# Attention block gated by a Mish MLP, one core: W1's last 18 tiles split beside the MLP's first chunk, attention's due times stretched there, a fourth buffer for Q/K results

## The chip, the cores and the metric

The kernel runs on one core of one Trainium2 chip. Five engines work from queues of their own: TensorE (PE: matmuls, PEld: weight loads), VectorE (DVE), ScalarE (ACT), GpSimd (POOL) and SyncE (SP, which issues most DMAs). The metric is device time in microseconds. The kernel before has three runs: 3395.11, 3398.99 and 3401.33 us, median 3398.99.

## The reference

```python
xn = layernorm(x)                                   # x: 1 x 2048 x 1024
q, k, v = split(xn @ wqkv)                          # 32 heads of 32
p = softmax(q @ k.T * 32 ** -0.5)                   # 2048 x 2048 for each head
s = concat(p @ v) @ wo
h = xn @ w1 + b1                                    # 1024 x 3584
g = silu((h * tanh(softplus(h))) @ w2)              # Mish between the two products
return x + s * g
```

All inputs are float32. The kernel keeps float32's precision by splitting each operand into a high and a low fp32r part: high is a copy that rounds, low is the difference. Three products (high high, high low, low high) are added up, so each logical product takes three matmuls.

## The kernel before

**Stages.** The layer norm, its transposes and V's products come first (to about 203 us). Then Q/K: 16 column blocks q = 0 to 15, seven products of 12 matmuls each (a scheme that needs seven products of halves in place of eight), whose results go through `qst` tiles to DRAM (`qs`, `ks`). Then attention and the MLP run interleaved (from about 558 us), and the output product `op` closes the program (from 3216 us).

**W1.** W1 has 28 tiles of 128 columns, each of 1024 rows in two halves. The MLP works on four chunks of 512 rows of x, so every tile is used four times: tile n of 112 is column tile n % 28. A tile is loaded in float32, split into high and low, and stored split to DRAM (`w1s`); `load_w1` loads it from there, 1 MB. The buffer ring `w1` has two places. In the kernel before, all 28 tiles are split ahead of the MLP:

- `W1_V` = 10 tiles in the V stage: `w1_early` loads one (`w1e`), and POOL makes both parts (`w1p`). It is called at ten of the V stage's steps and at two of those after it.
- the other 18 in Q/K: `presplit` takes half a tile at a time, 36 jobs, at three of the seven products of a block, except in blocks 6 to 8. It loads `praw`; three products later POOL casts it to `pw` and subtracts; one product later SP stores it to `w1s`.

**POOL in Q/K.** Besides those jobs, POOL makes the sums of Wqkv's halves (`ws`), and from the eleventh block on the low part of every second weight piece `wq`. It takes all of this in program order. TensorE's product waits for the low part of its `wq` at its third matmul.

**xr** is a 512-row operand of the products. It is loaded in four parts from `ts` just as Q/K starts. SP issues its DMAs in program order, too.

**Attention and MLP.** The order is made by a planner (`Plan`) when the kernel is built. It has a list of operations for each engine with an assumed duration, needs and buffer rings, and steps through a model of time; the order in which it issues them is the fixed order of each engine's queue on the chip. TensorE takes, of the operations that are ready, the one with the earliest due time, its `key`. Attention's keys (`s`, `t`, `pv`) run on `slot` for each step T (a head has 16 steps, 512 in all); the MLP's (`h`, `y`) on `tile_time` for each of the 112 tiles. `LEAN` is a string of digits, one for each 21 us of the model's time, that shifts keys by kind.

In a step of attention, TensorE makes `s` (for the row maxima, DVE `mx`) and `t` (transposed scores); ACT makes `p` = exp(t); POOL adds the p tiles up in `z`, which TensorE sums up in `zp` at the head's end; `pv` is the product with V. Seven `p` buffers lie between ACT and POOL. The head's result goes through one buffer, ring `on`, tag `on0`: ACT copies it there from PSUM, DVE scales it, SP stores it (`ot`) in four parts.

In the MLP, `h` takes 24 matmuls for a tile, the Mish goes over ACT and DVE, `y` takes another 24. W2 is split in the first chunk by `w2_op`: SP loads `w2r`, ACT makes the high part, POOL the low part, SP stores both (`w2s`); 56 of these half tiles.

Of the kernel before, what the change touches and what calls it, by code (L numbers as in the profile page):

```python
# [18 lines left out]
P = 128  # L19
# [7 lines left out]
W1_V = 10  # L27
# [23 lines left out]
LEAN = ("22007810058567756445438735813771770600785277035346426643654653488"  # L51
        "67323135577524547706646266273377660776675018744007005760023872000")
# [176 lines left out]
def body(ctx: ExitStack, tc: tile.TileContext, x, wqkv, wo, w1, b1, w2, out):  # L229
# [264 lines left out]
    for t in range(2, NT + 2):  # L494
# [32 lines left out]
        if t > 3 and t % 3:  # L527
            w1_early()
# [80 lines left out]
    for i, t in enumerate([4, 5, 6, 7, 12, 13, 14, 15, 0, 1, 2, 3, 8, 9, 10, 11]):  # L609
        v_group(1, t)()  # L610
        if i in (1, 3):
            w1_early()
# [107 lines left out]

    jobs = iter([(f, half) for f in range(W1_V, FT) for half in range(2)])

    def presplit():
        job = next(jobs, None)
        if job is None:
            return
        f, half = job
        raw = sp.tile([P, 512], F32, tag="praw", name=f"praw{f}_{half}", bufs=2)
        w = sp.tile([P, 2, 512], F32R, tag="pw", name=f"pw{f}_{half}", bufs=2)
        nc.sync.dma_start(raw.rearrange("p (k f) -> p k f", f=P),  # L730
                          w1[half * 512:half * 512 + 512, f * P:(f + 1) * P].rearrange("(k p) f -> p k f", p=P))

        def split():
            nc.gpsimd.tensor_copy(w[:, 0], raw)
            low(nc.gpsimd, w[:, 1], raw, w[:, 0])

        later.at(3, split)
        later.at(4, lambda: move(w1s[f][:, :, half * 4:half * 4 + 4], w.rearrange("p a (k f) -> p a k f", f=P)))
# [22 lines left out]
    def out_(q, half, chunk_, src):  # L761
        st = sp.tile([P, 2, 512], F32R, tag="qst", name=f"qst{q}_{half}_{chunk_}", bufs=3)
# [42 lines left out]

    q_load(1, ring_of(1))
    x_load(xr, ts[4])
# [71 lines left out]


# [6 lines left out]
    def s_stream():  # L887
        for h in range(1, H):
# [3 lines left out]
            for qt in range(NT):  # L892
                for kc in range(4):
# [10 lines left out]
                    m = Op("PE", MM, key=slot * (16 * (h - 1) + qt + (kc + 1) / 4 - LEAD), need=[loaded[h]],  # L904
# [59 lines left out]
    def t_stream():  # L964
        pts = {}
        for T in range(NS):
# [4 lines left out]
            for c in range(4):  # L971
# [14 lines left out]
                m = Op("PE", MM, key=slot * (T + (c + 1) / 4), emit=mm, take=["t", "b"], kind="t",  # L986
# [30 lines left out]
    def product(T, pts, size):  # L1017
# [18 lines left out]
        last_pv[h] = op("PE", PV * size, key=slot * (T + 1.5), need=need + [vt_[h]], emit=emit, col=True, kind="pv",  # L1036
# [52 lines left out]
    xts_ = {0: xc0}  # L1089

    def w1_op(n):
        def emit(at):
            load_w1(n)
        w1_ops[n] = op("SP", 0.1, emit=emit, take=["w1"], bytes_=P * 2 * KT * P * 4)
# [50 lines left out]
    def h_stream():  # L1145
        for n in range(NC * FT):
# [7 lines left out]
            for k in range(KT):  # L1154
                for a, b in THREE:
                    def mm(at, n=n, c=c, k=k, a=a, b=b, i=i, t=t):
                        if i == 0:
# [6 lines left out]
                           need=([w1_ops[n]] if n else []) + ([xc_ops[c, k // 2 * 2]] if c else []),  # L1164
# [342 lines left out]
```

## Time and profile before

| | |
|---|---|
| median of the three runs | 3398.99 us |
| the profiled execution: its own time | 3396.45 us |
| its span, first to last instruction | 3394.7 us |
| granted TensorE clock, mean | 0.996 |
| TensorE busy | 3354.4 us |
| POOL busy | 2556.3 us |
| DMA moved | 531.97 MB, mean 157 GB/s |

The profile is one execution. A line of the table of stretches has the stretch, its length, then for each engine busy us and instructions in brackets, the granted clock, the share of the DMA engines and GB/s. A line of the timeline has its start and length in us, engine, line, operation, output<-inputs and count; in square brackets stands how long the engine sat idle before it, and what ended that. A line of the groups has busy us, mean ns of one, then the idle time ahead of them and what ended it. The names are the program's, with numbers left out.

### The profile page before, as it was taken

How to read it: one execution, taken by the hardware profiler on the slowest of the kernel's cores; microseconds unless marked ns; L12 is line 12 of the kernel's file. 1: busy time of each engine (PE TensorE's matmuls, PEld its weight loads, DVE VectorE, ACT ScalarE, POOL GpSimd, SP SyncE). 2: the span in 40 equal slices, each digit the busy share in tenths (PEclk: the TensorE clock that was granted, in tenths of full speed). 3: DMA queues.
4: the chain of work that ended last, by engine and by line, in shares of the span. 5: the costliest groups of instructions: out<-in, count | busy, mean ns of one | idle time of the engine just before them, and what ended most of it. 6: DMA issues, size and time to landing. Idle time of an engine off the chain costs nothing.

```text
span 3394.7 us, 45896 instructions
## 1 busy us (share of the span) xinstructions
PE 3354.4 (99%) x16867; PEld 2460.3 (72%) x16867; DVE 2551.6 (75%) x3988; ACT 2037.3 (60%) x3272; POOL 2556.3 (75%) x789
## 2 busy tenths in 40 slices
PE   8999989999999999999999999999999999999999
PEld 7878767677777767777777777777777767777787
DVE  6776667887788777787788877878887787886543
ACT  5333324666766667666666676666676666666621
POOL 2445455899998999988888788888887888888800
PEclk9999999999999999999999999999999999999999
DMA  7978977434344463334333533343445343333482
GB/s 254 358 266 284 299 246 218 145 119 150 119 150 140 128 209 105 110 115 125 100 110 116 194 105 117 108 128 103 122 118 188 117 119 119 106 118 118 140 294 87
DMA packets 305732, 531.97 MB, mean 157 GB/s; under 512 B 88714, under 2 KB 151690, under 8 KB 283018
## 3 DMA queue, kind: packets, MB, share of 16 engines
q1 hardware_dynamic: 285796, 487.36, 45.8%
q10 hardware_dynamic: 19712, 41.69, 3.3%
q8 instruction: 133, 2.18, 0.3%
q14 instruction: 91, 0.75, 0.1%
HBM read 378.76 MB, written 149.16 MB: 156 GB/s over the span
## 4 chain that ended last, share of the span: by engine, by line
PE 91%; DMA 2%; DVE 2%; ACT 1%; issue 1%; POOL 0%; SPq 0%; ACTq 0%; DVEq 0%; POOLq 0%
PE y L1249 18%; PE h L1159 17%; PE t L978 14%; PE s L896 13%; PE pv L1025 13%; PE op L1348 5%; PE q_y L784 3%; PE v L351 2%; PE q_x L784 2%; PE q_z L784 2%; PE zp L1051 1%; DMA xc<-ts 1%; DVE mx L686 0%; DVE mx L902 0%; DMA w2r<-in_B_w_dram 0%
## 5 line engine op out<-in xcount | busy, mean ns | idle before, releaser
L1007 POOL TENSOR_TENSOR z<-z,p 128x2048 f32<-128x2048 f32 x448 | 2067.8, 4616 | 148.7 <-ACT p L282 123.1
L282 ACT ACTIVATE p<-t,zero 128x512 f32<-128x512 f32 x2048 | 1374.6, 691 | 502.2 <-PE t L978 481.6
L902 DVE TENSOR_REDUCE mx<-s 128x1 f32<-128x512 f32 x1984 | 1325.0, 686 | 420.6 <-PE s L896 412.3
L1249 PE MATMUL y<-w,act 128*128 128x512 f32 x2688 | 926.1, 391 | 2.2 <-ACT p L282 2.1
L978 PE MATMUL t<-qstack,kstack 128*128 128x512 f32 x2048 | 798.8, 393 | 0.9 <-DMA qstack<-mt 0.6
L896 PE MATMUL s<-kstack,qstack 128*128 128x512 f32 x1984 | 772.4, 393 | 0.8 <-DVE mx L902 0.5
L1159 PE MATMUL h<-xr,w 128*128 128x512 f32 x2016 | 702.6, 391 | 0.0
L1249 PEld LDWEIGHTS y<-w,act 128*128 128x128 f32 x2688 | 503.8, 188 | 111.5 <-issue 2.5
L978 PEld LDWEIGHTS t<-qstack,kstack 128*128 128x128 f32 x2048 | 383.0, 188 | 114.8 <-issue 22.0
L1025 PE MATMUL pv<-p,v 128*32 128x512 f32 x4096 | 459.2, 594 | 0.0
L896 PEld LDWEIGHTS s<-kstack,qstack 128*128 128x128 f32 x1984 | 370.2, 188 | 116.6 <-issue 24.5
L1159 PEld LDWEIGHTS h<-xr,w 128*128 128x128 f32 x2016 | 378.0, 188 | 81.1 <-issue 3.4
L1025 PEld LDWEIGHTS pv<-p,v 128*32 128x32 f32 x4096 | 123.8, 110 | 284.2 <-issue 282.1
L1271 DVE TENSOR_TENSOR yacc<-yacc,y 128x512 f32<-128x512 f32 x416 | 282.8, 681 | 38.1 <-PE y L1249 37.1
L1007 POOL TENSOR_TENSOR z<-p,p 128x2048 f32<-128x2048 f32 x32 | 147.8, 4620 | 184.8 <-PE zp L1051 145.8
L1159 PE MATMUL h<-xc,w 128*128 128x512 f32 x672 | 224.8, 391 | 0.1
L351 PE MATMUL v<-vw,xc 128*128 128x512 f32 x768 | 180.8, 394 | 1.5 <-DVE vw L293 1.5
L351 PEld LDWEIGHTS v<-vw,xc 128*128 128x128 f32 x768 | 143.1, 189 | 33.1 <-DVE vw L293 3.1
L1159 PEld LDWEIGHTS h<-xc,w 128*128 128x128 f32 x672 | 125.9, 188 | 26.5 <-ACT p L282 0.4
L784 PE MATMUL q_y<-xc,wq 128*128 128x512 f32 x480 | 122.0, 405 | 11.6 <-POOL wq L293 7.8
L285 ACT ACTIVATE act<-h 128x512 fp32r<-128x512 f32 x112 | 66.7, 595 | 102.2 <-DVE h L1208 100.7
L784 PEld LDWEIGHTS q_y<-xc,wq 128*128 128x128 f32 x480 | 93.9, 196 | 32.8 <-POOL wq L293 8.3
(140 smaller groups left out, 2989.3 us busy)
## 6 DMA issues: line engine op xcount, KB each, us to landing
w<-w1s SPq DMA_DIRECT2D x112, 1024.0 KB, 6.0
w<-w2s SPq DMA_DIRECT2D x168, 512.0 KB, 4.0
w2s<-w SPq DMA_DIRECT2D x56, 512.0 KB, 4.8
qstack<-qs SPq DMA_DIRECT2D x96, 256.0 KB, 6.9
kstack<-ks SPq DMA_DIRECT2D x96, 256.0 KB, 6.1
w1s<-pw SPq DMA_DIRECT2D x36, 512.0 KB, 3.4
qs<-qst ACTq DMA_DIRECT2D x32, 512.0 KB, 3.1
ks<-qst ACTq DMA_DIRECT2D x32, 512.0 KB, 4.8
```

What stands on the lines that cost most here:

```text
L282: nc.scalar.activation(out_, in_, fn, bias=zero if bias is None else bias, scale=scale)
L351: nc.tensor.matmul(ps, xc[t // 4][k // HK][:, a, k % HK, (t % 4) * P:(t % 4 + 1) * P], vw[i, k // 2][:, b, k % 2], start=n == 0, stop=n == ...
L784: nc.tensor.matmul(ps, w[:, a, k], xx[:, b, k], start=m == 0 and i in (0, 1, 4), stop=m == 3 * HK - 1, skip_group_check=i not in (0, 1, 4))
L896: nc.tensor.matmul(sp_, qst[h % 3][:, qt * P:(qt + 1) * P], kst[h % 3][:, kc * 512:(kc + 1) * 512], start=True, stop=True)
L902: nc.vector.reduce_max(tiles["mx"][:, qt, kc:kc + 1], tiles[qt, kc], axis=AX.X)
L978: nc.tensor.matmul(tp, kst[h % 3][:, kt * P:(kt + 1) * P], qst[h % 3][:, c * 512:(c + 1) * 512], start=True, stop=True)
L1007: nc.gpsimd.tensor_tensor(zs[h], pts[T - 1] if kt == 1 else zs[h], pts[T], ALU.add)
L1025: nc.tensor.matmul(pv[h][c * DH:(c + 1) * DH, :], vt[h][:, k, :], pts[T - kt + k][:, c * 512:(c + 1) * 512], start=k == 0, stop=k == NT - 1)
L1159: nc.tensor.matmul(t["h"], w1t[n][:, a, k], xts_[c][k // HK][:, b, k % HK], start=i == 0, stop=i == 3 * KT - 1)
L1249: nc.tensor.matmul(t["y"], acts[n][:, p, s * P:(s + 1) * P], w2t[m_][:, q], start=j == 0 and i == 0, stop=j == YB - 1 and i == 2)
L1271: nc.vector.tensor_tensor(ya, ya, t["y"], ALU.add)
L1348: nc.tensor.matmul(ps[t, dh], ohl[t // 4, k][:, a, s * P:(s + 1) * P], wt[k][:, b, r], start=k == 0 and i == 0, stop=k == KT - 1 and i == 2)
```

## The change

Four things. `W1_V` goes from 10 to 4, so that the V stage splits four tiles at six steps; `presplit` does the tiles 4 to 9, 12 half tiles, all in blocks 0 to 3, with one `pw` buffer in place of two. The tiles 10 to 27 are split by `w1_op` in the MLP's first chunk, half a tile at a time: SP loads 256 KB to the buffer of the heads' outputs (`on0`, now also `w1r`), ACT makes the high part in the tile itself, POOL the low part, and once both halves are through, SP stores the tile to `w1s` for the three chunks that follow. The tile's first use needs no load from `w1s`. `h` waits for each half apart.

Attention's keys go through `due`: below 600 us of the model's time they are stretched by 1.25, and the rest is pressed together so that the end stays. `LEAN` has new digits.

`qst` gets four buffers, three before. And `xr` is loaded ahead of block 1's raw weights instead of behind them.

```diff
-W1_V = 10
+W1_V, W1_Q = 4, 10
+
+SLOW, UNTIL = 1.25, 600.0
...
-LEAN = ("22007810058567756445438735813771770600785277035346426643654653488"
-        "67323135577524547706646266273377660776675018744007005760023872000")
+LEAN = ("17005811310607050748168705630685764600685277038346416663654556688"
+        "64343135546528545608186210263377657666375628744007405708070872000")
...
-        if t > 3 and t % 3:
+        if t > 3 and t % 3 == 2:
             w1_early()
...
-        if i in (1, 3):
+        if i == 1:
             w1_early()
...
-    jobs = iter([(f, half) for f in range(W1_V, FT) for half in range(2)])
+    jobs = iter([(f, half) for f in range(W1_V, W1_Q) for half in range(2)])
...
-        w = sp.tile([P, 2, 512], F32R, tag="pw", name=f"pw{f}_{half}", bufs=2)
+        w = sp.tile([P, 2, 512], F32R, tag="pw", name=f"pw{f}_{half}", bufs=1)
...
-        st = sp.tile([P, 2, 512], F32R, tag="qst", name=f"qst{q}_{half}_{chunk_}", bufs=3)
+        st = sp.tile([P, 2, 512], F32R, tag="qst", name=f"qst{q}_{half}_{chunk_}", bufs=4)
...
+    x_load(xr, ts[4])
     q_load(1, ring_of(1))
-    x_load(xr, ts[4])
...
+    def due(T):
+        t = slot * T
+        if t < UNTIL:
+            return t * SLOW
+        return UNTIL * SLOW + (t - UNTIL) * (total - UNTIL * SLOW) / (total - UNTIL)
...
-                    m = Op("PE", MM, key=slot * (16 * (h - 1) + qt + (kc + 1) / 4 - LEAD), need=[loaded[h]],
+                    m = Op("PE", MM, key=due(16 * (h - 1) + qt + (kc + 1) / 4 - LEAD), need=[loaded[h]],
...
-                m = Op("PE", MM, key=slot * (T + (c + 1) / 4), emit=mm, take=["t", "b"], kind="t",
+                m = Op("PE", MM, key=due(T + (c + 1) / 4), emit=mm, take=["t", "b"], kind="t",
...
-        last_pv[h] = op("PE", PV * size, key=slot * (T + 1.5), need=need + [vt_[h]], emit=emit, col=True, kind="pv",
+        last_pv[h] = op("PE", PV * size, key=due(T + 1.5), need=need + [vt_[h]], emit=emit, col=True, kind="pv",
...
+    w1r, w1_kept = {}, {}
 
     def w1_op(n):
         def emit(at):
             load_w1(n)
-        w1_ops[n] = op("SP", 0.1, emit=emit, take=["w1"], bytes_=P * 2 * KT * P * 4)
+        need = [w1_kept.get(n - 2)]
+        if not W1_Q <= n < FT:
+            w1_ops[n, 0] = w1_ops[n, 1] = op("SP", 0.1, need=need, emit=emit, take=["w1"], bytes_=P * 2 * KT * P * 4)
+            return
+        a = None
+        for half in range(2):
+            r = slice(half * HK, half * HK + HK)
+
+            def raw(at, half=half):
+                if half == 0:
+                    w1t[n] = w1_tile(f"w1_{n}")
+                w1r[n, half] = att.tile([P, 512], F32, tag="on0", name=f"w1r_{n}_{half}").rearrange("p (k f) -> p k f", f=P)
+                nc.sync.dma_start(w1r[n, half], w1[half * 512:half * 512 + 512, n * P:(n + 1) * P].rearrange("(k p) f -> p k f", p=P))
+
+            def high(at, half=half, r=r):
+                copy(w1t[n][:, 0, r], w1r[n, half])
+
+            def rest(at, half=half, r=r):
+                low(nc.gpsimd, w1t[n][:, 1, r], w1r[n, half], w1t[n][:, 0, r])
+
+            b = op("SP", 0.1, need=[a] + need, emit=raw, take=["on"] if half else ["w1", "on"], bytes_=P * 512 * 4)
+            a = op("ACT", 0.6, need=[b], emit=high)
+            w1_ops[n, half] = op("POOL", 1.3, need=[a], emit=rest, give=["on"], key=-1)
+        w1_kept[n] = op("SP", 0.1, emit=lambda at: move(w1s[n], w1t[n]), need=[w1_ops[n, 0], w1_ops[n, 1]], bytes_=P * 2048 * 4)
...
-                           need=([w1_ops[n]] if n else []) + ([xc_ops[c, k // 2 * 2]] if c else []),
+                           need=([w1_ops[n, k // HK]] if n else []) + ([xc_ops[c, k // 2 * 2]] if c else []),
```

Four places show how the queues move. First POOL in Q/K, at the eleventh block, where it makes the low part of the weight piece `wq40`. Before:

```order
L548 TENSOR_TENSOR ws4_3586<-spare_3271 128x512
L548 TENSOR_TENSOR ws1_3588<-ws4_3586,spare_3271 128x512
L548 TENSOR_TENSOR ws3_3594<-spare_3271 128x512
L734 CAST pw20_1_3546<-praw20_1_3545 128x512
L293 TENSOR_TENSOR pw20_1_3546<-praw20_1_3545,pw20_1_3546 128x512
L548 TENSOR_TENSOR ws6_3636<-spare_3271,ws1_3588 128x512
L734 CAST pw21_0_3601<-praw21_0_3600 128x512
L293 TENSOR_TENSOR pw21_0_3601<-praw21_0_3600,pw21_0_3601 128x512
L293 TENSOR_TENSOR wq40_3722<-ws3_3594,wq40_3722 128x512
```

Now:

```order
L550 TENSOR_TENSOR ws4_3482<-spare_3187 128x512
L550 TENSOR_TENSOR ws1_3484<-ws4_3482,spare_3187 128x512
L550 TENSOR_TENSOR ws3_3490<-spare_3187 128x512
L550 TENSOR_TENSOR ws6_3526<-spare_3187,ws1_3484 128x512
L295 TENSOR_TENSOR wq40_3602<-ws3_3490,wq40_3602 128x512
```

The two W1 jobs between the sums and `wq40` are gone. Second, SP as Q/K starts (`vs` is V's result, `raw` are Wqkv's columns). Before:

```order
L357 DMA vs1_79<-vst1_11_1925 128x512
L540 DMA raw2_1961<-in_A_wqkv_dram 128x8x128
L540 DMA raw3_1962<-in_A_wqkv_dram 128x8x128
L289 DMA xr_1958<-ts4_140 128x2x512 x4
L730 DMA praw10_0_1990<-in_B_w1_dram 128x4x128
```

Now:

```order
L359 DMA vs1_79<-vst1_11_1877 128x512
L291 DMA xr_1910<-ts4_140 128x2x512 x4
L542 DMA raw2_1913<-in_A_wqkv_dram 128x8x128
L542 DMA raw3_1914<-in_A_wqkv_dram 128x8x128
L732 DMA praw4_0_1942<-in_B_w1_dram 128x4x128
```

The four loads of `xr` have passed the two raw loads. Third, POOL in the MLP's first chunk, at the start of head 3's sum `z3`. Before, one W2 split stands there for every two or three adds; now:

```order
L295 TENSOR_TENSOR w1_14_7178<-w1r_14_0_7179,w1_14_7178 128x512
L295 TENSOR_TENSOR w2_25_7232<-w2r_25_7233,w2_25_7232 128x512
L295 TENSOR_TENSOR w1_14_7178<-w1r_14_1_7336,w1_14_7178 128x512
L1015 TENSOR_TENSOR z3_7361<-p48_7182,p49_7241 128x2048
L295 TENSOR_TENSOR w2_26_7341<-w2r_26_7342,w2_26_7341 128x512
L1015 TENSOR_TENSOR z3_7361<-z3_7361,p50_7350 128x2048
L1015 TENSOR_TENSOR z3_7361<-z3_7361,p51_7390 128x2048
L295 TENSOR_TENSOR w2_27_7433<-w2r_27_7434,w2_27_7433 128x512
L295 TENSOR_TENSOR w1_15_7461<-w1r_15_0_7462,w1_15_7461 128x512
L1015 TENSOR_TENSOR z3_7361<-z3_7361,p52_7431 128x2048
```

The halves of tiles 14 and 15 stand between the adds. Fourth, TensorE where the MLP's second chunk begins with `h28` (the number behind `t` is the step T). Before:

```order
L1159 MATMUL h27_10937<-xc0_1_178,w1_27_10663 128x512
L896 MATMUL s9_6_2_11237<-kstack0_3437,qstack0_3436 128x512
L978 MATMUL t126_2_11240<-qstack1_3442,kstack1_3443 128x512
L1159 MATMUL h28_11248<-xr1_0_11005,w1_28_10928 128x512
L896 MATMUL s9_6_3_11250<-kstack0_3437,qstack0_3436 128x512
```

Now:

```order
L904 MATMUL s7_12_2_10379<-kstack1_3353,qstack1_3352 128x512
L1191 MATMUL h27_10139<-xc0_1_178,w1_27_9963 128x512
L986 MATMUL t103_1_10384<-qstack0_3346,kstack0_3347 128x512
L1191 MATMUL h28_10386<-xr1_0_10239,w1_28_10089 128x512
L904 MATMUL s7_12_3_10392<-kstack1_3353,qstack1_3352 128x512
```

The MLP's first chunk now ends 23 steps of attention sooner. The number of matmuls is the same in both, and so is the number of groups of `pv` and `zp`, 96. Between the first matmuls of `h10` and `h28` the order now holds 1397 matmuls of `h`, `y`, `s` and `t` and 64 steps of `pv`.

## Prediction

> **What bounds the kernel now.** I read the page's busy shares first, then the groups of TensorE for the price of one matmul, then a table of stretches, and last the waits and the timeline inside the stretches that lose time.
>
> ```profile
> PE 3354.4 (99%) x16867; PEld 2460.3 (72%) x16867; DVE 2551.6 (75%) x3988; ACT 2037.3 (60%) x3272; POOL 2556.3 (75%) x789
> 3216.26 174.09 PE op L1348 x768
> ```
>
> The first line is the page's, the second is one of the chain of waits. TensorE is busy nearly throughout, and 768 matmuls in a row took 174.09 us: 0.2267 us each, with every operand at hand. The change adds no matmul and takes none away, so only time in which matmuls stand still, or run slower than 0.2267 us, can be won or lost. Where is that? The table of stretches (busy us and instructions of each engine, granted clock, DMA share, GB/s):
>
> ```profile
> 203.00:230.00 27.00, 23.39 (x89) 17.61 (x88) 12.30 (x15) 6.83 (x12) 8.11 (x6) 0.87 0.99 321
> 230.00:358.00 128.00, 128.00 (x566) 105.81 (x566) 82.94 (x106) 44.81 (x79) 68.77 (x58) 1.00 0.91 295
> 358.00:390.00 32.00, 27.57 (x110) 21.98 (x108) 18.04 (x24) 9.74 (x17) 10.67 (x8) 0.89 1.07 366
> 390.00:435.00 45.00, 45.00 (x198) 36.84 (x197) 29.17 (x37) 15.81 (x28) 26.76 (x22) 1.00 0.76 222
> 435.00:452.00 17.00, 9.15 (x31) 7.06 (x30) 4.97 (x8) 1.63 (x3) 10.38 (x10) 0.70 0.75 249
> 452.00:558.00 106.00, 101.20 (x425) 79.77 (x424) 83.42 (x121) 28.95 (x56) 56.54 (x48) 0.98 0.73 229
> 558.00:610.00 52.00, 48.32 (x230) 34.38 (x229) 43.03 (x69) 36.41 (x63) 38.01 (x12) 1.00 0.64 196
> 610.00:1110.00 500.00, 499.81 (x2595) 354.73 (x2594) 408.92 (x653) 349.14 (x566) 460.12 (x137) 1.00 0.44 135
> 1110.00:3200.00 2090.00, 2089.31 (x10880) 1489.62 (x10879) 1636.10 (x2585) 1409.87 (x2232) 1787.09 (x421) 1.00 0.41 125
> ```
>
> Q/K runs from 203 to 558 us. A stretch's loss is its length less 0.2267 us for each matmul: 27 - 89 x 0.2267 = 6.8 us; 230:358 and 390:435 lose nothing; 358:390 loses 32 - 24.9 = 7.1; 435:452 loses 17 - 7.0 = 10.0; 452:558 loses 106 - 96.3 = 9.7. That is 33.6 us in Q/K. From 610 to 3200 us TensorE idles 0.9 us in all: there is nothing to win there, only to lose. So the question is how much of the 33.6 us the change takes back, and what it puts into the 2,600 us that have no gap.
>
> ```profile
> PE q_y L784 <- POOL wq L293: 7.8, 1, 7.8
> PE q_y L784 <- DMA xr<-ts: 3.5, 3, 1.9
> PE s L682 <- ACT mt L285: 2.4, 3, 0.9
> PE y L1249 <- ACT p L282: 2.1, 1, 2.1
> ```
>
> These waits of TensorE (total us, times, longest) name the places.
>
> **The change, part by part.** *435:452, the stall behind W1's split.*
>
> ```profile
> 432.05 1.14 ACT L285 ACTIVATE wq<-ws 128x512 fp32r<-128x512 f32 x2
> 436.14 0.61 PE L784 MATMUL q_y<-xc,wq 128*128 128x512 f32 x2
> 441.38 0.61 POOL L734 CAST pw<-praw 128x512 fp32r<-128x512 f32 x1 [14.49 <-DMA praw<-in_B_w_dram]
> 443.29 1.26 POOL L293 TENSOR_TENSOR wq<-ws,wq 128x512 fp32r<-128x512 f32 x1
> 444.61 4.63 PE L784 MATMUL q_y<-xc,wq 128*128 128x512 f32 x10 [7.85 <-POOL wq L293]
> ```
>
> The product's third matmul needs the low part of wq, which POOL computes. POOL had a W1 split in front of it and sat 14.49 us until praw landed. The change does 12 such half-tile jobs instead of 36, three in each of the products q = 0 to 3, so none is left behind 280 us (203 + 28 x 2.72 us, twelve matmuls each). Without it, the high part was there at 433.2 us, POOL's 1.26 us end near 434.5, and the third matmul was due at 436.6: 2.1 us in hand. I take 9.5 of the 10.0 us (bounds 0, if POOL's sums wait for their own load there, and 10.0). The ten matmuls after the stall took 4.63 us instead of 2.27. The Trainium skill (TensorE: Matmul & The Clock Gate, "Part 1: The HAM clock gate") says that an idle window of some 3.4 us halves the clock and about as long a busy one restores it; that would put the cost behind the stall at 1.7 us, where the rows have 2.4, and the whole loss here would be 9.3 instead of 10.0. By that window, waits well below 3.4 us would cost no clock, and the row at 538 us below contradicts it.
>
> *203:230, xr.*
>
> ```profile
> 209.13 1.01 SPq L540 DMA_DIRECT2D raw<-in_A_wqkv_dram  x2
> 210.25 3.40 SPq L289 DMA_DIRECT2D xr<-ts  x4
> 214.46 0.61 ACT L285 ACTIVATE wq<-raw 128x512 fp32r<-128x512 f32 x1
> 218.46 0.93 PE L784 MATMUL q_y<-xr,wq 128*128 128x512 f32 x3 [1.85 <-DMA xr<-ts]
> 212.52 11.42 DMA xr<-ts
> ```
>
> The last row is from the chain of waits: the load's time to its landing at 223.9. xr's four loads now go ahead of the two raw loads. That is 1.1 us earlier on SP, and 1 MB less ahead of them at 321 GB/s, 3.3 us: 4.4 us. SP was also held at 209.13 by the raw loads' own conditions. The product with xr was due near 216.6 us, its last quarter of three matmuls 2.0 us later, at 218.6, and that quarter landed at 223.9: 5.3 us too late, of which 4.4 or more go. Clock and idle together cost 6.8; I take 6.0 (bounds 0 and 6.8). The price is that raw comes about 4 us later. ACT's copy from it at 214.46 then waits, and behind that copy stand ACT's evacuations; the product that reads it was due at 203 + 7 x 2.72 = 222.0 us, so nothing is lost.
>
> *358:390, the loads for the second half of the products.*
>
> ```profile
> 360.38 11.35 DMA xc<-ts
> ...
> 372.27 0.60 ACT qst L285
> 372.87 1.04 ACT wq L285 x2
> ...
> 375.49 5.46 PE q_y L784 x12
> ```
>
> Here the chain runs from an xc load's landing to ACT's store of a result and on to wq. That load belongs to products in which no W1 job runs, before or after. A fourth qst buffer frees the copy at 372.27, but the store in front of it on ACT waits for the load all the same. I take 0.5 (bounds 0 and 3.5, the wait without its slow clock).
>
> *452:558, the first scores between the products.*
>
> ```profile
> 538.19 4.44 PE L784 MATMUL q_y<-xc,wq 128*128 128x512 f32 x12
> L293 DVE TENSOR_TENSOR wq<-ws,wq 128x512 fp32r<-128x512 f32 x53 | 52.2, 994 | 18.4 <-ACT wq L285 18.3
> ```
>
> The waits (s on mt and on mx) are chains of ACT and DVE with no W1 job in them; they stay. But DVE's subtraction from SBUF averages 994 ns while POOL works beside it. I take 2.0 of the 9.7 us (bounds 0 and 5). Twelve matmuls took 4.44 us at 538, 1.7 us over their price, after waits below 1 us each. The Trainium skill (SBUF — State Buffer, "Who interferes with whom") gives the reason why DVE should gain: POOL and DVE share a port pair, held for a whole instruction. No row isolates it here.
>
> *The V stage* loses five of its ten early W1 steps and one of the two later ones.
>
> ```profile
> L351 PE MATMUL v<-vw,xc 128*128 128x512 f32 x768 | 180.8, 394 | 1.5 <-DVE vw L293 1.5
> ```
>
> At most 1.5 us can come back; I take 0.5. One pw buffer instead of two holds POOL's cast until the previous half's store has landed, in q = 0 to 3, where TensorE loses nothing behind xr; 0 (bounds 0 and 3: at most three sums of POOL come late by a store, and they are made a product or more ahead).
>
> Sum of the gains: 9.5 + 6.0 + 0.5 + 2.0 + 0.5 = 18.5 us.
>
> *The MLP's first chunk pays.* Thirty-six halves are loaded, copied by ACT, subtracted by POOL there.
>
> ```profile
> L1007 POOL TENSOR_TENSOR z<-z,p 128x2048 f32<-128x2048 f32 x448 | 2067.8, 4616 | 148.7 <-ACT p L282 123.1
> L293 POOL TENSOR_TENSOR w<-w2r,w 128x512 fp32r<-128x512 f32 x56 | 72.3, 1291 | 37.8 <-ACT w L285 37.4 <-PE s L896 0.4
> L285 ACT ACTIVATE w<-w2r 128x512 fp32r<-128x512 f32 x56 | 35.4, 632 | 29.8 <-DMA w2r<-in_B_w_dram 29.7
> w2r<-in_B_w_dram SPq DMA_DIRECT2D x56, 256.0 KB, 3.7
> praw<-in_B_w_dram SPq DMA_DIRECT2D x36, 256.0 KB, 6.4
> L1025 PE MATMUL pv<-p,v 128*32 128x512 f32 x4096 | 459.2, 594 | 0.0
> ```
>
> POOL: 36 x 1.29 = 46 us more where it is busy 92% (460 of 500 us). The stretched due times take that back: in the order, h28 starts with t103, before with t126; 23 steps fewer, each 15/16 x 4.62 = 4.33 us of POOL, make 100 us. The chunk also gets shorter: between h10 and h28 the order holds 1397 matmuls of h, y, s and t and 64 steps of pv, 317 + 64 x 0.897 (459.2 us, pv's busy time, over 512 steps) = 374 us, 21 us a tile. So POOL stays as full as it was. The 23 steps come later: (1787 + 100) / 2090 = 90% there, still under the 92% at which TensorE lost nothing; 0 (bounds 0 and 3).
>
> Two things can hold TensorE. First, ACT works in order and sits until a late raw lands. For W2 there were 56 such copies and 29.7 us of ACT's waiting, and TensorE lost 2.1 us once (y on ACT p, above); 36 more make 1.3 us. Second, h waits for its split. A half takes 3.7 (landing) + 0.63 + 2.31 (half of a z-add ahead of it on POOL) + 1.29 = 7.9 us, two of them through one buffer 15.9, against 21 us a tile: 5 us in hand. At praw's 6.4 us and a whole z-add it is 25.9: 4.9 us late. SP stands still meanwhile, since the second half's load waits for POOL's first; behind it queue W2's raws, the heads' stores and their stacks. I take 1.2 us here, about as much again, since W2's rows are the nearest: 2.5 with the first (bounds 0, and 14.7 for three tiles at the worst; nothing below zero beyond the 3.7 us that 558:610 idles).
>
> 18.5 - 2.5 = 16.0 us. The profiled execution took 3396.45 us, so its like would take 3380.5; the median shown, 3398.99, stands 2.5 us higher. Forecast: **3383 us**.
>
> **Rivals.** *Given back.* Q/K gains 18.5, and six of the 18 tiles come 2.5 us late: 3399 - 18.5 + 15 = 3395.5. For it: POOL and SP in order, with waits on each other. Against it: 56 such chains cost 2.1 us.
>
> *Slower.* One buffer (that of the heads' outputs, which a head's output also takes) makes the two halves a chain longer than a tile. It decides from 25.3 us, 1.4 us a tile; halfway to the worst, 2.5 us on all 18, it gives 3399 - 18.5 + 45 = 3425. For it: landings of 6.4 us in a full stretch. Against it: the DMA share is 0.44 here, and the raws are issued a whole tile ahead.
>
> *The wait moves.* At 435 us POOL's sums wait for spare's load instead, so wq is late all the same: 3399 - 16 + 9.5 = 3392.5, at the edge of what can be told. Against it: those sums ran at 418 to 425 us, ahead of the stalled cast.
>
> *More than that.* The quieter queues free 358:390 and 452:558 too, say three quarters of the 14.3 us left there: 3399 - 16 - 10.7 = 3372. For it: DMA shares of 1.07 and 0.73 there. Against it: neither wait has a W1 job in its chain.
>
> **How the numbers follow.** Forecast 0.57, given back 0.17, slower 0.13, moved 0.08, more 0.05. The forecast's own range is 3374 to 3391: the terms' bounds, not all at the same end. A measurement tells 0.2%, 6.8 us, from no change. Faster by that is below 3392.2: 0.56 + 0.04 + 0.05 = 0.65. Within: 0.01 + 0.17 + 0.04 = 0.22. Slower: 0.13. The range of 3370 to 3402 holds all but the slower rival and the tails, under 0.2.
>
> **What would show it.** Right: Q/K ends 16 to 20 us sooner; no wait of q_y on POOL at q = 11; xr's wait under 1 us; the 358:390 stall still there; TensorE idle from 560 to 1110 us under 7 us, with waits of h on POOL's w few. Wrong: the 7.85 us back under another releaser; h waiting on w tile after tile, or z and p waits of TensorE as POOL passes 96%; any idle time behind 1110 us above 4 us.

## The result, and the profile after

| | before | after |
|---|---|---|
| median of the runs | 3398.99 us (3395.11 to 3402.75, 5 runs) | 3385.16 us (3382.31 to 3386.54, 5 runs) |
| profiled execution: its own time / span | 3396.45 / 3394.7 us | 3385.16 / 3383.4 us |
| TensorE busy | 3354.4 us | 3350.0 us |
| POOL busy | 2556.3 us | 2524.8 us |

The ratio is 0.9958 with a 95% interval of 0.9944 to 0.9973: faster by 0.4%, and the whole interval lies below 1. The two profiled executions differ by 11.3 us.

Where did these come from? First the borders of the program's stages after the change. The first two rows are of the timeline (start and length in us): the first Q/K product and the first score of attention. The row of "op", the last 768 matmuls, is of the chain of waits.

```profile
201.19 2.88 PE L786 MATMUL q_x<-xc,wq 128*128 128x512 f32 x12
...
547.89 0.62 PE L904 MATMUL s<-kstack,qstack 128*128 128x512 f32 x2
```

```profile
3204.97 174.10 PE op L1380 x768
```

Before, the timeline has these two at 202.84 and 558.33 us, and the chain has op at 3216.26. So the V stage ends 1.65 us sooner; Q/K takes 346.7 us instead of 355.5, which is 8.8 us less; and attention with the MLP takes 0.85 us less than before, although the eighteen splits were put into it. The gain lies in Q/K, but Q/K gained half of the 18.0 us that were forecast.

Next the table of stretches for TensorE alone, after (stretch, length, busy us and matmuls, granted clock, DMA share, GB/s):

```profile
210.00:235.00 25.00, 22.63 (x99) 1.00 0.92 282
235.00:297.00 62.00, 61.24 (x268) 1.00 0.86 267
297.00:320.00 23.00, 19.28 (x76) 0.93 0.67 212
...
357.00:390.00 33.00, 27.75 (x109) 0.90 1.04 354
390.00:450.00 60.00, 59.49 (x263) 1.00 0.63 191
450.00:530.00 80.00, 76.53 (x327) 1.00 0.46 145
530.00:548.05 18.05, 18.05 (x81) 1.00 0.47 142
```

And the stretches of before, cut at the same places as far as they compare:

```profile
210.00:235.00 25.00, 21.39 (x80) 0.86 1.01 313
297.00:320.00 23.00, 23.00 (x103) 1.00 0.80 263
357.00:390.00 33.00, 28.57 (x114) 0.90 1.07 363
434.00:453.00 19.00, 11.15 (x40) 0.73 0.76 251
453.00:530.00 77.00, 73.78 (x313) 1.00 0.77 240
530.00:558.33 28.33, 26.75 (x109) 0.94 0.60 198
```

The loss of a stretch is again its length less 0.2267 us for each matmul. At 435 us it went from 9.9 to at most 0.4 (390:450): that stall is gone. 210:235 went from 6.9 to 2.6. The last stretches (453:530 with 530:558.33, now 450:530 with 530:548.05) went from 9.7 to 5.6. 357:390 went from 7.2 to 8.3. And **297:320, which had lost nothing, now loses 5.8 us** (103 matmuls before, 76 after), with another 1.2 in 235:297. This new stall ate most of what the old one gave back.

The timeline of the changed kernel shows it. POOL first, then SP, then TensorE:

```profile
299.78 0.61 POOL L736 CAST pw<-praw 128x512 fp32r<-128x512 f32 x1 [4.14 <-DMA w1s<-pw]
...
301.72 1.29 POOL L550 TENSOR_TENSOR ws<-raw 128x512 f32<-128x512 f32 x1
```

```profile
295.67 0.52 SPq L291 DMA_DIRECT2D w1s<-pw  x1
296.28 1.68 SPq L542 DMA_DIRECT2D raw<-in_A_wqkv_dram  x2
```

```profile
305.08 0.73 PE L786 MATMUL q_y<-xc,wq 128*128 128x512 f32 x2 [1.20 <-ACT wq L287]
306.20 2.56 PE L786 MATMUL q_y<-xc,wq 128*128 128x512 f32 x10 [0.39 <-DVE wq L295]
310.90 4.25 PE L786 MATMUL q_x<-xc,wq 128*128 128x512 f32 x12 [2.13 <-ACT e L287]
```

Read from the bottom: q_x and q_y wait for ACT, ACT for POOL's sums ws. POOL could not begin these before 301.72, for two reasons that came together. It had sat 4.14 us until the store of the half before had left the one pw buffer, and then had its own half to make (to 301.7). And raw, which the sums read, was issued only at 296.28 and landed 5.39 us later: on SP it stood behind that same store of the half before, issued at 295.67, which itself had waited for POOL's subtraction (to 295.64). With one buffer every half waits for the store of the one before, and SP's loads wait with it.

The other stall, that of 357:390, in the chain of waits after the change:

```profile
362.01 12.98 DMA xc<-ts
...
375.07 0.37 ACTq L291
...
375.48 0.60 ACT qst L287
376.08 1.05 ACT wq L287 x2
...
378.71 5.47 PE q_y L786 x12
```

It is the chain of before, a little longer: an xc load lands, ACT issues the store of a result, and only then come the next cast and the weights that q_y needs. The semaphores in the trace (the counters by which a DMA reports that it has landed) say why the store stands behind a load. Up to 560 us the program's DMAs use eight of them in turn. The store at 375.07 uses the one that the xc load of 362.01 used before it. ACT's queue waits on that semaphore until 375.01, and the last part of the load was counted there at 374.99.

On balance attention paid nothing that TensorE shows. The page of the profile has less idle time in front of POOL's z additions than before (148.7 us then), and the waits of TensorE from 550 to 1110 us add up to 3.3 us, with none of h on POOL's w:

```profile
L1015 POOL TENSOR_TENSOR z<-z,p 128x2048 f32<-128x2048 f32 x448 | 2066.8, 4613 | 106.4 <-ACT p L284 77.3
```

```profile
PE t L986 <- ACT p L284: 1.1, 1, 1.1
PE t L986 <- DMA qstack<-mt: 1.0, 1, 1.0
...
PE h L1191 <- ACT p L284: 0.3, 1, 0.3
```

### The profile page after: what moved, and what is told of

Its sections match the earlier page's. It is cut to its first block, busy times and chain, and to the rows that moved or that the text cites. A ratio compares the mean times of both kernels' runs of the same rounds, so it can differ in the third digit from the quotient of the medians.

```text
span 3383.4 us, 45816 instructions
## 1 busy us (share of the span) xinstructions
PE 3350.0 (99%) x16867; PEld 2458.7 (73%) x16867; DVE 2526.9 (75%) x3988; ACT 2057.3 (61%) x3308; POOL 2524.8 (75%) x753
## 4 chain that ended last, share of the span: by engine, by line
PE 92%; DMA 2%; DVE 2%; issue 1%; ACT 1%; POOL 1%; SPq 0%; ACTq 0%; POOLq 0%; DVEq 0%
PE y L1281 18%; PE h L1191 17%; PE t L986 14%; PE s L904 13%; PE pv L1033 13%; PE v L353 5%; PE op L1380 5%; PE q_y L786 2%; PE q_x L786 2%; PE q_z L786 1%; PE zp L1059 1%; POOL z L1015 1%; DMA raw<-in_A_wqkv_dram 1%; DVE mx L688 0%; DVE wq L295 0%
## 5 line engine op out<-in xcount | busy, mean ns | idle before, releaser
L1191 PE MATMUL h<-xr,w 128*128 128x512 f32 x2016 | 695.1, 391 | 0.0
```

Of the source, the lines that this page charges most:

```text
L1191: nc.tensor.matmul(t["h"], w1t[n][:, a, k], xts_[c][k // HK][:, b, k % HK], start=i == 0, stop=i == 3 * KT - 1)
```

## The experiments

Each was measured against the kernel before in the same session; the ratios compare across sessions. Experiments 1 to 4 ran together, then 5, 6 and 9, then 7, 8, 10 and 11. In the second of these sessions the changed kernel itself ran again as the mark:

> The changed kernel itself once more, beside the others on the same chip and with the same runs of the kernel before, as the mark that the experiments are measured against: a ratio of 0.995 to 0.997. If it comes out below 0.9950, the gains of the experiments so far are smaller than they look; theory and rivals say nothing else of it.

It took 3383.93 us, ratio 0.9957 (0.9945 to 0.9968), span 3384.7 us. Its profile is called the change's second profile below.

There is one profile of each version, so the spread of equal code matters. The change, its second profile and experiments 9 to 11 have the same Q/K code. From the first product to the first score they take 343.7 to 348.1 us, and their 210:235 holds 92 to 102 matmuls, which is 2.3 us. A difference between two profiles that is smaller than these is not shown.

**1. The two buffer counts exchanged again.**

```diff
-        w = sp.tile(... tag="pw", name=f"pw{f}_{half}", bufs=1)
+        w = sp.tile(... tag="pw", name=f"pw{f}_{half}", bufs=2)
-        st = sp.tile(... tag="qst", name=f"qst{q}_{half}_{chunk_}", bufs=4)
+        st = sp.tile(... tag="qst", name=f"qst{q}_{half}_{chunk_}", bufs=3)
```

> The change with its two buffer counts in the Q/K stage exchanged again: two buffers for the split halves of W1, three for the Q/K results. Theory (one buffer for the split halves): POOL's cast waits for the store of the half before (30 us in 201:330 of the changed kernel), the sums of the weights stand behind it, and so 297:320 loses 5.8 us and 235:297 1.2 us. Both go: some 3379 us, 297:320 with about 101 matmuls in its 23 us instead of 76, waits of POOL on the W1 stores under 5 us. Rival 1 (late weights: the load of raw stands on SP behind a W1 store that waits for POOL, with one buffer or two): the loss of 297:320 stays, about 3385 us. Rival 2 (the fourth result buffer is what removed the stall of 435 us): 435:452 loses some 8 to 10 us again, 3388 us or more.

3376.25 us, ratio 0.9943 (0.9931 to 0.9955), span 3376.6 us. The stretches of this version:

```profile
297.00:320.00 23.00, 23.00 (x104) 1.00 0.48 160
...
357.00:390.00 33.00, 27.44 (x110) 0.90 0.90 307
```

The stall at 300 us is gone, and Q/K takes 339.6 us, below the spread of the change. (The two intervals of the times overlap; it is the stretch that shows the difference.) The waits of POOL between 201 and 330 us (total us, times, longest), first of the change, then of this version:

```profile
POOL pw L736 <- DMA w1s<-pw: 21.1, 7, 6.9
POOL pw L736 <- DMA qs<-qst: 9.3, 1, 9.3
```

```profile
POOL pw L736 <- DMA praw<-in_B_w_dram: 12.7, 4, 5.8
```

The second row names a result store, but this releaser is inferred. By the semaphores in the trace that cast waited, like the others, for W1's store: the one of 284.09, whose last part landed at 293.19, just ahead of the cast at 293.34. So POOL had waited 30.4 us for W1's stores, and now waits for none. SP's loads of raw, which the change issued at 296.28, come ten microseconds sooner:

```profile
285.85 3.97 SPq L542 DMA_DIRECT2D raw<-in_A_wqkv_dram  x2
```

So the late raw load (rival 1) was no cause of its own, but the same one seen on SP. Rival 2 falls too: with three result buffers 390:450 holds 261 matmuls and loses 0.8 us, so it was not the fourth buffer that removed the stall of 435 us. This run alters two counts at once. Experiment 2 keeps four result buffers and has no stall at 300 us, so these alone do not make it; two buffers for the halves beside four for the results were not run.

**2. No split in Q/K at all**: six tiles go back to the V stage, the eighteen stay in the first chunk.

```diff
-W1_V, W1_Q = 4, 10
+W1_V, W1_Q = 10, 10
-        if t > 3 and t % 3 == 2:
+        if t > 3 and t % 3:
-        if i == 1:
+        if i in (1, 3):
```

> The change with no W1 tile split in the Q/K stage: the six that were split there are split in the V stage again, as before the change; the twelve later calls, the first chunk and the orders stay. Theory (the splits themselves hold POOL in Q/K): 297:320 gets its 5.8 us back, 235:297 its 1.2 us, and the small waits of 450:548 may shrink; the V stage gives back its 1.8 us: some 3380 us. Rival (late weights are a matter of the DMA queues, not of the splits): 297:320 still loses over 3 us, and the V stage's loss comes on top: 3387 us.

3379.39 us, ratio 0.9953 (0.9940 to 0.9965), span 3377.6 us. The first product begins at 203.06, 1.9 us later than in the change: that is what the V stage's gain was made of. The stretches:

```profile
210.00:235.00 25.00, 21.50 (x89) 0.93 0.91 269
...
297.00:320.00 23.00, 23.00 (x104) 1.00 0.43 137
```

235:297 holds 275 matmuls and 297:320 holds 104, so nothing is lost there, as the theory has it. 210:235 holds 89 matmuls and loses 4.8 us, with xr ahead of raw but the V stage of before; no profile with the lighter V stage has so few. 450:530 holds 328 matmuls, as in the change, so the rest of the loss there has nothing to do with the splits.

**3. The weights of q=1 loaded ahead of xr again.**

```diff
-    x_load(xr, ts[4])
     q_load(1, ring_of(1))
+    x_load(xr, ts[4])
```

> The change with one line moved back: the weights of q=1 are loaded ahead of xr, as before the change. Theory (the order of these two loads made the gain of 210:235, 4.3 us net: 6 us of waiting for xr gone, about 2 us of waiting for late weights come): 210:235 loses 6 to 7 us again, of it 5 to 6 us before the first q_y matmul on xr; some 3389 us. Rival (what helped xr was the lighter DMA traffic after the V stage and the earlier start): the wait for xr stays under 2 us and the weights come in time, 3383 to 3385 us.

3382.76 us, ratio 0.9959 (0.9945 to 0.9972): no difference from the change that can be told. Here is the wait for xr in this version, where before the change it was 3.5 us:

```profile
PE q_y L786 <- DMA xr<-ts: 2.6, 3, 1.7
```

210:235 holds 91 matmuls, a loss of 4.4 us; the change had 2.6 in one profile and 4.1 (92 matmuls) in the other. The rival has the time right. Its bound of 2 us for the wait does not hold: the order does take the wait for xr away, but in these profiles late weights cost about as much. Of the 4.3 us that 210:235 gained, 2.5 are there without the new order.

**4. The result stores of q=7 and q=8 issued by SP instead of ACT.**

```diff
-        later.at(1, lambda: move(dst, st, nc.scalar))
+        later.at(1, lambda: move(dst, st, nc.sync if q in (7, 8) else nc.scalar))
```

> The change with the result stores of q=7 and q=8 issued by SP instead of ACT. Theory (at 375 us ACT stands at the issue of a store, 6.2 us, which may start only when an earlier xc load of SP's has landed, and the cast of wq for the next q_y stands behind it): ACT's wait and the 5.0 us wait of q_y at 378 go, some 3380 us. Rival 1 (the store's wait goes to SP and holds the loads behind it there, so that the next pieces come late instead): 357:390 still loses 7 to 9 us, 3385 us or up to 5 us more. Rival 2 (the xc tiles themselves are late, since the DMA engines are full, 354 GB/s): q_y waits for DMA xc instead of ACT, 3384 to 3386 us.

3376.70 us, ratio 0.9944 (0.9931 to 0.9956), span 3376.6 us.

```profile
357.00:390.00 33.00, 30.36 (x134) 1.00 1.06 359
```

134 matmuls instead of 109, at about the same DMA traffic (359 GB/s, 354 in the change): the loss fell from 8.3 to 2.6 us, and Q/K takes 340.9 us, again below the spread of the change. The full DMA engines (rival 2) were not the cause; ACT standing at the issue of a store was.

**5. Both mends together (1 and 4).**

> Both mends of the Q/K stage in one: two buffers for the split halves of W1 and three for the results, and the result stores of q=7 and q=8 issued by SP. Theory (two separate causes: POOL's cast behind one buffer at 300 us, ACT's store behind SP's load at 375 us): the gains add up. Against the changed kernel the first gained 6.8 us of span and the second 6.8; of each some 1 us lies elsewhere, so 11 to 13 us together: a span near 3371, no loss in 297:320 and under 4 us in 357:390. Rival 1 (the stall of 375 is one of DMA bandwidth; with the W1 stores on time again it comes back, as waits for xc or raw): 357:390 loses over 6 us, 3375 to 3377 us. Rival 2 (one takes the other's place, since with three result buffers the store that SP holds back keeps ACT from the next result): as much, with ACT's waits for DMA on qst.

3384.8 us, ratio 0.9960 (0.9948 to 0.9973), span 3383.3 us: as slow as the change. The theory falls; the gains do not add up. ACT, TensorE and SP in this version's timeline:

```profile
377.36 0.60 ACT L287 ACTIVATE qst<-q_z 128x512 fp32r<-128x512 f32 x1 [15.85 <-DMA ks<-qst]
```

```profile
380.58 4.62 PE L786 MATMUL q_y<-xc,wq 128*128 128x512 f32 x12 [14.38 <-issue]
```

```profile
362.53 6.22 SPq L542 DMA_DIRECT2D raw<-in_A_wqkv_dram  x2
368.85 4.14 SPq L291 DMA_DIRECT2D ks<-qst  x2
```

297:320 is whole (103 matmuls), but 357:390 holds only 74. ACT waits 15.85 us for a store of ks to land, since that store's tile is the third and last result buffer. SP could not issue the store before 368.8 us, because the loads stood ahead of it. This is rival 2, at over twice the price that it named (16.2 us lost in 357:390, where it had over 6). So the fourth result buffer, which experiment 1 did not miss, is just what lets the stores go to SP.

**6. As 5, with the weights of q=1 between xr's second and third load.**

```diff
-    x_load(xr, ts[4])
-    q_load(1, ring_of(1))
+    for k in range(HK):
+        move(xr[:, :, k], ts[4][:, :, k])
+        if k == 1:
+            q_load(1, ring_of(1))
```

> The version before it in this call, with the weights of q=1 loaded between the second and the third of xr's four loads. Theory (xr and the weights of q=1 share one queue of loads, and whichever stands last is late; loading the weights first left 2.6 us of waiting for xr, xr first left 2.3 us of waiting behind late weights): the middle way gains 1 to 2 us in 210:235, 3369 to 3370 where the one before has 3371. Rival (the loss of 210:235 is the sum of the DMA traffic, in whatever order): the same time within 0.7 us, and 210:235 loses over 2.5 us.

3382.55 us, ratio 0.9957 (0.9944 to 0.9969), span 3380.7. The expected level was off, for the reason above. Against 5, 210:235 holds 101 matmuls instead of 95, which is 1.4 us and in the theory's favour; but equal code gives 92 to 102 there, and the times can't tell the two apart either. So the theory is not shown.

**7. One ring of five for halves and results, stores of q=7 and q=8 on SP.** Five buffers are the memory of one and four.

```diff
-        w = sp.tile(... tag="pw", name=f"pw{f}_{half}", bufs=1)
+        w = sp.tile(... tag="qst", name=f"pw{f}_{half}", bufs=5)
-        st = sp.tile(... tag="qst", name=f"qst{q}_{half}_{chunk_}", bufs=4)
+        st = sp.tile(... tag="qst", name=f"qst{q}_{half}_{chunk_}", bufs=5)
-        later.at(1, lambda: move(dst, st, nc.scalar))
+        later.at(1, lambda: move(dst, st, nc.sync if q in (7, 8) else nc.scalar))
```

> The change with one ring of five buffers for both the split halves of W1 and the Q/K results (instead of one and four, the same memory), and the stores of q=7 and q=8 on SP. The halves are used in q=0 to q=3 alone, so that from q=4 on five buffers stand for the results. Theory (in the version that had two and three buffers with stores on SP, ACT waited 15.9 us for a store of ks to land because the third result buffer was not free; with four it had not; and at 300 us a second buffer for the halves is what POOL's cast lacks): both stalls are gone, 297:320 and 357:390 lose under 0.5 and under 3 us, span 3369 to 3373. Rival 1 (the stores on SP delay the loads behind them, whatever the buffers): 357:390 still loses over 6 us, 3376 us or more. Rival 2 (halves and results hold each other up in one ring): 235:320 loses over 3 us, 3374 to 3378 us.

3372.13 us, ratio 0.9930 (0.9916 to 0.9943), span 3369.5 us. Both stretches are as the theory says, and Q/K takes 333.3 us:

```profile
297.00:320.00 23.00, 23.00 (x103) 1.00 0.51 171
...
357.00:390.00 33.00, 30.29 (x133) 1.00 0.96 323
```

**8. As 7, with the loads as in 6.**

> The version before it in this call with the weights of q=1 loaded between the second and the third of xr's four loads. Theory (late weights and late xr share the loss of 210:235; with two and three buffers it went from 3.5 to 2.1 us): 1 to 2 us less than the version before it, 3368 to 3371. Rival (that difference was chance between two executions): the same within 0.7 us.

3370.36 us, ratio 0.9924 (0.9910 to 0.9937), span 3366.9 us, and 103 matmuls in 210:235 instead of 99. Its median is the lowest of all, ahead of both kernels: its interval ends below where that of the change begins. Its lead over version 7, 1.8 us in the times and 1.7 us in Q/K, is within the spread, so this order of the loads is not shown to gain anything.

**9. The change without the stretch.** So far all lay in Q/K. Why did the eighteen splits cost the first chunk nothing?

```diff
-SLOW, UNTIL = 1.25, 600.0
+SLOW, UNTIL = 1.0, 600.0
```

> The change with the due times of attention not stretched (factor 1 instead of 1.25); the eighteen tiles are still split in the first chunk. Theory (stretching makes the room on POOL: in 600:1100 it does 81 z additions instead of 89, which saves 37 us of 4.62 each, for 34 low halves of W1 that take 44 us): without it POOL needs some 505 of the 500 us there and stands at 97 to 100%, the halves of W1 or the z additions come late, h or t waits, and the first chunk loses 4 to 10 us: 3389 to 3395 us where the change has 3385, with waits of h on POOL w in the list. Rival (the planner's order follows the engines anyway, and POOL had slack enough): POOL under 97%, the first chunk as with the stretch, 3383 to 3387 us.

3421.32 us, ratio 1.0069 (1.0057 to 1.0082). Without the stretch the change would have been a loss: 37.4 us over the mark, where the theory gave 10 at most. POOL was busy 464.6 of the 500 us from 600 to 1100, under the 97% that the theory named. So the splits without the stretch do cost time, as it says, but POOL was not as full as it says.

**10 and 11. The table of leanings of before, with and without the stretch.** The table was fitted to one plan, so it has to be taken out of the comparison:

```diff
-LEAN = ("17005811310607050748168705630685764600685277038346416663654556688"
-        "64343135546528545608186210263377657666375628744007405708070872000")
+LEAN = ("22007810058567756445438735813771770600785277035346426643654653488"
+        "67323135577524547706646266273377660776675018744007005760023872000")
```

> The change with the table of leanings from before it; stretch and splits stay. With the unstretched kernel that kept the new table (37 us slower than the change, and of that only some 7 us in 600:1100) and with the next run this makes a table of four: stretch or not, new table or old. Theory (the stretch by itself makes the room for the splits on POOL): within 8 us of the change, 3378 to 3393 us, TensorE's share in 600:1100 over 99.3%. Rival (stretch and table were fitted to one another; a table that fits another plan costs tens of us anywhere in the program): 3400 to 3430 us, with most of the loss behind 1100 us.

> The change with the table of leanings from before it and no stretch: the plan of before, with the eighteen splits put into it. Theory (the splits have no room on POOL without the stretch: 89 z additions of 4.62 us, 42 low halves of W2 and 34 of W1 of 1.30 us make some 510 of 500 us in 600:1100): slower than the run before it by 8 us or more, of which most in 600:1100 and just behind it, POOL over 95% there. Rival 1 (the stretch is worth nothing, the plan makes room by itself): within 5 us of the run before it. Rival 2 (the fit of table and plan decides): over 3400 us for both.

| | stretch 1.25 | no stretch |
|---|---|---|
| new table | 3383.93 us, 0.9957 | 3421.32 us, 1.0069 |
| old table | 3400.85 us, 1.0016 (1.0007 to 1.0025) | 3416.33 us, 1.0060 (1.0047 to 1.0073) |

With the old table the stretch is worth 15.5 us, and with the stretch the new table is worth 17 us by the times and 20 by the ratios (these two ran in different sessions). The first run came out as its rival says, the second as its theory says (14.3 of its 15.5 us lie in 560:1100, below), only that POOL stands at 93%, not over 95. The second run's rival 2, over 3400 us for both, was met too, by 0.85 us in one of them. The change needed the stretch and the table.

The list of waits names about half of this loss: behind 560 us TensorE's listed waits add up to 4 us in the change, and to 10 to 21 in the others. So I took the start times of TensorE's matmuls from 560 to 3203 us and counted the neighbours (none of them a pv) that start more than 0.29 us apart; the excess is what they take beyond 0.2267 us each.

```
                            pairs   excess us   of it 560 to 1100   1100 to 1600   behind
before                        172        31.6                11.3            6.3     14.1
change (second profile)       169        29.9                 7.5            5.6     16.8
old table, stretch            242        45.9                11.7           10.8     23.5
old table, no stretch         270        60.8                26.0           13.9     20.9
new table, no stretch         276        62.3                20.4           16.0     25.9
```

The excess over the change is 16.0, 30.9 and 32.4 us. From the first score to the end the three profiled executions take 17.6, 34.3 and 37.5 us longer than the change's second profile, so the excess is some nine tenths of it. The splits without stretch and new table cost 26.0 - 11.3 = 14.7 us in the chunk in which they stand and as much again behind it. The stretch takes back the former, the table most of the latter.

What the late matmuls wait behind, the runs don't prove. A candidate stands in ACT's waits from 560 to 1100 us. First the change's second profile, then the old table without the stretch:

```profile
ACT w L287 <- DMA w2r<-in_B_w_dram: 14.4, 9, 2.9
ACT w L287 <- DMA w1r<-in_B_w_dram: 14.2, 7, 3.9
```

```profile
ACT w L287 <- DMA w1r<-in_B_w_dram: 32.9, 10, 6.5
ACT w L287 <- DMA w2r<-in_B_w_dram: 28.3, 13, 5.9
```

ACT works in order and stands at a raw half that has not landed for 61.2 us instead of 28.6, with its casts and exponentials (p, act) behind it. With the stretch and the old table it is 22.4, before the change 22.9, and with the new table and no stretch 47.7. So the two plans without the stretch, which have by far the largest excess in this stretch, have the longest waits here as well. That the one comes of the other is argued, not shown: TensorE's own listed waits name DVE's `mx` most in the old table without the stretch (6.9 us of s). And no run shows which step holds the raw halves up, the one buffer, SP behind it or POOL's z additions; that stays open.

## Why the prediction was right, and where its terms were not

The forecast of 3383 us was 2 us from the measured 3385.16, and it named the right stage. But its sum of 16.0 us is right only because terms that were off on both sides cancelled, which was luck:

| term | forecast, us | measured, us | from |
|---|---|---|---|
| stall behind W1's split at 435 us | 9.5 | 9.6 | 434:453, now in 390:450 |
| xr | 6.0 | 4.3 | 210:235 |
| one pw buffer | 0 | -7.7 | 235:320 |
| 358:390 | 0.5 | -1.1 | 357:390 |
| 452:558 | 2.0 | 4.1 | last two stretches |
| V stage | 0.5 | 1.65 | start of the first product |
| MLP's first chunk | -2.5 | 0.85 | first score to op |
| sum | 16.0 | 11.7 | spans: 11.3 |

The measured column is from one profile each, and equal Q/K code spreads over 4.3 us in sum, so the small terms are rough. The row of the first chunk has all of attention and the MLP in it.

**435 us**: as forecast, in place and size; no wait of q_y on POOL is left there.

**One pw buffer, "0 (bounds 0 and 3)"**: this is the step that failed. It argued that POOL's sums come late by one store and are made a product or more ahead. The runs show a loop through two queues: POOL's cast waits for the store, the store waits on SP for POOL's split, and raw waits on SP behind the store. The longest of POOL's waits for a W1 store was 9.3 us, over three times the 2.72 us of the one product that it counted on. The loop cost 7.7 us here, and experiment 1, which undid it, removed the stall.

**xr**: the wait went, as said, but "nothing is lost" by the later raw was wrong. After the change the chain has a load of raw that took 11.96 us, to 219.55, then POOL's sums and ACT's copies, and q_z and q_x late. By experiment 3 the order of the loads is worth nothing that the times can tell. Part of the gain in this stretch has another source, the V stage, which ends sooner and with fewer stores of W1. Of the 6.9 us lost before, 4.8 stay with the new order and the V stage of before (experiment 2), and 4.4 with the old order and the new V stage (experiment 3). With a spread of 2.3 us in equal code, how the 4.3 us divide between the two stays open.

**358:390**: the place and the chain were read rightly, and it stayed. The fourth buffer did not help because, as the prediction says, the store in front waits for the load all the same; experiment 4 shows that this wait can be moved off ACT, which takes 5.7 us off the loss.

**452:558 and V** were undersized, by 2.1 and 1.2 us. In the first, version 2 with no split at all has the same loss as the change in 450:530, and so has version 1 with three result buffers; what is left is that no split runs there any more. The prediction took a reason from the Trainium skill (SBUF — State Buffer, "Who interferes with whom"), the port that POOL and DVE share. The traces agree that such a cost exists: in Q/K before the change, DVE's subtractions for wq took 686 ns on average where no POOL instruction ran beside them (36, none over 695) and 1237 ns where one did (45). But only 8 of them lie in 452:558, so whether the 4.1 us are theirs stays open.

**The first chunk**: the size was near (forecast 2.5 us of loss, measured 0.85 of gain), but by luck again. The prediction reckoned with POOL's busy share, 36 x 1.29 us against 100 us set free by the stretch, and with waits of h. It had no term for the new table, which turned out to be worth 17 to 20 us. The landing of w1r, median 5.3 us, fell inside its bounds of 3.7 and 6.4, and no wait of h on a split is listed. Yet the splits were by no means nearly free: without the stretch and the new table they cost some 30 us. In size that lies between "given back" and "slower" among the rivals, though not by their mechanism, the late halves for h. Two other parts of the same change paid for it: the stretch, on which the prediction had counted, and the table, on which it had not. POOL's share would not have told: it is 93% in the slow plan too.

```profile
600.00:1100.00 500.00, 491.37 (x2484) 345.70 (x2476) 401.49 (x637) 342.02 (x557) 467.35 (x160) 0.99 0.50 148
```

This is the stretch of the old table without the stretched due times; POOL's 467.35 us are those of the change (469.00), while TensorE does 2484 matmuls instead of 2551. Behind 1100 us POOL is at 1823.88 of 2090 us, 87%, where the prediction had 90%.

**The clock.** The prediction doubted the window of some 3.4 us that the Trainium skill gives (TensorE: Matmul & The Clock Gate, "Part 1: The HAM clock gate"). The changed kernel bears the doubt out: at 310.90 twelve matmuls took 4.25 us instead of 2.72, at a granted clock of 0.67 from there to 315.20, after waits of 1.20, 0.39 and 2.13 us, each well short of the window. How much idle time in how long a stretch it takes, no run here isolates.

**The list of signs**: Q/K ended 10.4 us sooner instead of 16 to 20, and that was the warning; the other signs came as listed.

## What to carry to other kernels

Before a double buffer is reduced to one, follow its release through every in-order queue: a store on SP that waits for POOL holds the loads behind it, and these loads feed POOL. Two stalls that are mended one by one need not add up, since a mend may draw on the buffer that the other gave away (experiments 1, 4 and 5); a ring shared by tiles that live at different times gave both. And where a plan, its due times and a fitted table change in one step, price the added work with the old plan too: the engine's busy share hid a cost of 30 us that the stretch and the table had paid.

## What the runs showed of the hardware that was not expected

What a wait costs behind it does not grow with its length here: after 2.13 us of idling (and two shorter waits just before) the next twelve matmuls took 1.53 us more than 2.72, after 4.99 us (the change at 378.71) 2.75 more, and after 14.38 us (version 5) 1.90 more.

A store that ACT issues can be held by a load that SP issued: at 375 us ACT stood 6.2 us until an xc load had landed, since the two report on one semaphore in turn, and with the store on SP that wait left ACT (experiment 4). The two queues are not independent in this program.

In attention, where TensorE is listed as busy over 98% in every version, plans differ by 30 us through gaps of about 0.2 us each between single matmuls. The lists of waits show about half of that; the start times show it.
